# Memory attention and two MLPs: key-value sums in eight places of the array, and other changes to the start

## The chip, the cores and the metric

The kernel runs on one core of one Trainium2 chip, in one launch. The metric is the device time of one execution in microseconds, the median of several runs; lower is better.

## The reference

Four batches, eight heads, 576 tokens, 64 values a head, 32 memory slots. All data is float32.

```
a    = softmax(phi over tokens)            # phi: 4 x 8 x 576 x 32
k_m  = a^T k ;  v_m = a^T v                # 32 x 64 a head
attn = softmax(q k_m^T / 8 over the 32)    # 576 x 32 a head
x    = attn v_m                            # joined over heads: 2304 x 512
h    = x w_in ;   g = max(0.01 h, h) ;     x  = g w_out     # w_in 512 x 2048, w_out 2048 x 512
h    = x w_in2 ;  g = h tanh(softplus h) ; out = g w_out2
```

The weights come in 64-bit floats and are decoded on the chip from their two 32-bit words.

## The kernel before, in words

**Stages.** Heads are taken in two groups of four. For a batch and a group, `kv_first` (batch 0) or `kv_tasks` (the others) loads phi, keys and values, subtracts the maximum over tokens, takes the exponential, and sums a^T k and a^T v on TensorE; `kv_norm` divides by the token sums (a scaled copy called kvn) and transposes. `score_tasks` loads and transposes queries, multiplies them with the keys (`scores`) and does the softmax over 32 slots in two halves of 288 tokens (`half`, nearly all on VectorE). `vw_tasks` multiplies v_m with a chunk of w_in, so that the first layer works straight on the softmax. The first layer then runs over items (`stage1`): one block of 128 hidden columns times one half of a batch's tokens; each item has six matmuls (L1044) and, behind the activation, twelve with w_out (L1077). A weight piece of w_in (w0 to w3 are the first chunk) or of w_out (`wo_unit`) is loaded raw, decoded on ScalarE and VectorE, and split in a rounded part and a rest. The second MLP (L1398 and L1551) takes the second half of the time.

**Batch 0.** Its layout puts head h of a group on partitions 32h to 32h + 31, each partition with 18 tokens. The sums are 72 matmuls of 32 x 32 weights and 128 columns (keys and values side by side), 18 for each head; head h uses rows 32h and columns 32h of the array, so four places lie on the diagonal. Each float32 matmul stands in the trace as two instructions. The token sums are made on VectorE (`fold`: a reduction, a 32 x 32 transpose, a reduction).

**Order.** Nothing is ordered by hand. Each step is a task with a priority, an estimated duration on each engine that could do it, the tasks that it waits for and the buffers that it takes. `Order.run` is a list scheduler that goes through estimated time when the program is built; what it picks becomes the fixed order of each engine's queue. A lower priority number goes first. `K['O']` gives the order of batch 0's loads on the SP queue, which issues all transfers. `K['FILL']` counts filler matmuls (L874) for an idle TensorE early on. `T` gives the turns: batch 0 with chunk 0 and then 1 of w_in, then batch 1, and so on. Loads of batch 1 wait for batch 0's buffers of phi, keys, values and queries of group 0; group 1 has its own in a side pool. PSUM has eight buffers: acc0 to acc3, h0, h1 and two misc.

Of the kernel before, what the change touches and what calls it, by code (L numbers as in the profile page):

```python
# [9 lines left out]
F32 = mybir.dt.float32  # L10
# [4 lines left out]
ALU = mybir.AluOpType  # L15
AX = mybir.AxisListType
# [7 lines left out]
def hop(a, b):  # L24
# [5 lines left out]

K = dict(
    LAG1=2, WIN=8, OB=2, RS=4, FILL=36, A1=10, S1=2.8,
    A2=30, S2=2.6, V1=2.4, V2=14, W2=56.0, W2S=3.8, O='phi0 kv0 phi1 q0 w0 kv1 q1 w1 w2 w3', HF0=-20.0, HF1=-7.0,
    HFD=0.3, TOP=0.3, HI=0.2, WO=2.0, WOL=1, WC=3.0, WC0=-38.0, V0=3.0, COLD=20, GL=1.5, AL=5.0, XL=22.0, T='0:1 0:1 1:2 0:2 1:2', SB=1,
    DW=280e3, DQ=1.3, DP=1.2, DS=0.78, DI=0.38, L4=0.5, L4P=1.6, L4S=0.8, L4T=5.0, MA=6, FK=-52.5, DWF=0.85, MV="......rvvrrvvrvr",
)


# [121 lines left out]
def kernel(  # L160
# [111 lines left out]
    make_identity(nc, ident)  # L272
    ones = const.tile([P, PR], F32, name="ones")
    nc.vector.memset(ones, 1.0)
    sched = Order()

    def dma(**args):
# [21 lines left out]
    def act(n, ps=False):  # L299
        return n / 1196 + (0.051 if ps else 0.093)  # L300
# [126 lines left out]
    def kv_first(g, p0, dp):  # L427
        sp = "s" if g else ""
        ph = tags["phi" + sp].new([P, 576] if sp else [P, HG * R * M])
        kv = tags["kv" + sp].new([P, 2304] if sp else [P, 2 * HG * R * D])  # L430
        phv = lambda: ph.t[:, :576].rearrange("p (r m) -> p r m", m=M)
        hs = slice(g * HG, (g + 1) * HG)
        l_phi = add(
            {"SP": K["DS"] * mb(294912)}, PPHI[g],
            lambda e: (ph.make(), dma(out=phv(), in_=phi[0, hs].rearrange("h (p r) m -> (h p) r m", r=RQ))), (), [ph],
        )

        def ld(e):
# [24 lines left out]

        t1 = add({"DVE": 2.8}, p0, fmax, [l_phi], [rm, mx], [ph])
        t2 = add(
            {"ACT": act(576)}, p0 + 2 * dp,
            lambda e: nc.scalar.activation(out=ph.t[:, :576], in_=ph.t[:, :576], func=AF.Exp), [t1], (), [ph],
        )
        den, rec = tags["den" + sp].new([P, 1]), tags["rec" + sp].new([P, 1])

        def fden(e):
            fold(ALU.add, den.make())
            nc.vector.tensor_scalar(out=den.t, in0=den.t, scalar1=1e-9, scalar2=None, op0=ALU.add)
            nc.vector.reciprocal(out=rec.make(), in_=den.t)

        t3 = add({"DVE": 1.9}, p0 + 3.5 * dp, fden, [t2], [den, rec], [ph, rm])
        acc = acc_tag.slots[2 * g].new([P, 2 * D])

        def fkv(e, r0):
            if not r0:  # L480
                acc.make()
            for r in range(r0, r0 + RQ // 3):
                for h in range(HG):
                    rows = slice(M * h, M * (h + 1))
                    nc.tensor.matmul(  # L485
                        out=acc.t[rows, :].rearrange("p (j d) -> p j d", j=2),
                        lhsT=phv()[rows, r, :],
                        rhs=kv.t[rows, :2304].rearrange("p (j r d) -> p j r d", j=2, r=RQ)[:, :, r, :],
                        start=(r == 0),
                        stop=(r == RQ - 1),  # L490
                    )

        t4 = None
        for r0 in range(0, RQ, RQ // 3):
            t4 = add(
                {"PE": 1.4}, K["FK"] if g else p0 + 3.8 * dp, lambda e, r0=r0: fkv(e, r0), [t2, l_kv, t4], [] if t4 else [acc],
                [ph, kv, acc] if t4 else [ph, kv],
            )
        return acc, rec, t4, t3

    def kv_tasks(b, g, p0, dp):
# [4 lines left out]
        kv = tags["kv" + sp].new([P, 2, HG, R, D])  # L506
        hs = slice(g * HG, (g + 1) * HG)
        pl = p0 - 6
        l_phi = load(pl, ph.make, lambda: phi[b, hs].rearrange("h (p r) m -> p h r m", p=PR), 294912, (), [ph], (), K["DP"])

        def ld(e):
            kv.make()
            for j, x in enumerate((k, v)):
                dma(out=kv.t[:PR, j], in_=x[b, hs].rearrange("h (p r) d -> p h r d", p=PR))

        l_kv = add({"SP": K["DQ"] * mb(1179648)}, pl + 0.2, ld, (), [kv])

        def fold(buf, op):

# [90 lines left out]
    def kv_norm(b, g, p0, dp, acc, rec, t7, t8):  # L610
        sp = "s" if b < K['SB'] and g == 1 else ""
        kvn = tags["kvn" + sp].new([P, 2 * D])

        def fn(e):
            if e == "ACT":
                nc.scalar.activation(out=kvn.make(), in_=acc.t, func=AF.Copy, scale=rec.t)
            else:
                nc.vector.tensor_scalar(out=kvn.make(), in0=acc.t, scalar1=rec.t, scalar2=None, op0=ALU.mult)

        t9 = add({"ACT": act(P, True), "DVE": dve(P)}, p0 + 4.3 * dp, fn, [t7, t8], [kvn], [acc, rec])  # L620
        kt = (misc if b else acc_tag.slots[1]).new([P, P])
# [23 lines left out]
    def score_tasks(b, g, pq, ps, dp):  # L645
        sp = b < K['SB'] and g == 1
        qT = (qT_s if sp else qT_tag).new([P, HG, NB1])
        parts, firsts_q = [], []
# [11 lines left out]
                    in_=q_g[h].rearrange("(j p r) d -> p j (r d)", r=2, p=32),  # L660
                )

        lq = add({"SP": (K["DQ"] if b else K["DS"]) * mb(589824)}, pq - 4 if b else PQ[g], ld, (), [qb])
        for i in range(3):
            ps_b = (misc if b else h_tag).new([P, 3, P])

# [53 lines left out]
    def half(b, g, hf, ps, dp, qT, parts, a, ab, both):  # L720
# [50 lines left out]
    win, win_ready, w_scr = {}, {}, {}  # L771

    def vw_tasks(b, c, p0):

# [884 lines left out]
```

## Time and profile before

| | us |
|---|---|
| median of 3 runs | 750.35 (749.92 to 750.53) |
| the profiled execution | 751.77 |
| its span, first to last instruction | 750.0 |
| PE busy | 737.4 (98%) |
| DVE busy | 545.8 (73%) |
| ACT busy | 413.1 (55%) |
| transfers | 183.75 MB, mean 245 GB/s |

PE is TensorE, PEld its weight loads, DVE VectorE, ACT ScalarE, SP the engine whose queue issues transfers. An "idle before" names the time for which an engine stood still and what ended it. [...] The stretch before 40 us holds batch 0's attention and the first weights; nearly all the rest is the two MLPs, in which batches 1 to 3 are prepared beside the matmuls.

### The profile page before, as it was taken

The page shows a single profiled execution, that of the slowest core. Times are in us where ns is not written, and L with a number is a line of the kernel's source. Part 1 is how long each engine was busy: PE and PEld are TensorE (multiplying, and loading weights), DVE is VectorE, ACT ScalarE, POOL GpSimd, SP SyncE. Part 2 cuts the span into 40 slices and gives each one's busy share as a digit, 9 for nine tenths or more (in the row PEclk, how much of TensorE's full clock was granted, in tenths as well). Part 3 has the DMA queues.
Part 4 walks back from the last instruction along what each step waited for, and adds up shares of the span by engine and source line. Part 5 has one row for each costly group of instructions (what it writes and reads, how often), then busy time and mean ns, then how long its engine had stood idle before and what let it go on. Part 6 is the DMA issues. An engine that isn't in the chain of part 4 may idle for free.

```text
span 750.0 us, 15892 instructions
## 1 busy us (share of the span) xinstructions
PE 737.4 (98%) x5978; PEld 706.4 (94%) x5978; DVE 545.8 (73%) x1180; ACT 413.1 (55%) x916; POOL 0.7 (0%) x6
## 2 busy tenths in 40 slices
PE   8899999999999999999999999999999999999997
PEld 7689899988898998999999999999999999999997
DVE  6989758768676886655779798767576965665585
ACT  3867457646464656554456674644455644454443
POOL 0000000000000000000000000000000000000000
PEclk9999999999999999999999999999999999999999
DMA  9984595838869397966269988788977878987476
GB/s 345 294 286 136 176 285 169 245 122 263 239 222 320 141 300 241 308 193 215 99 247 317 351 321 293 226 265 258 322 250 245 266 246 254 290 289 224 126 214 193
DMA packets 99436, 183.75 MB, mean 245 GB/s; under 512 B 8224, under 2 KB 55328, under 8 KB 99360
## 3 DMA queue, kind: packets, MB, share of 16 engines
q1 hardware_dynamic: 99360, 182.75, 75.8%
q8 instruction: 47, 0.77, 0.4%
q14 instruction: 29, 0.24, 0.1%
HBM read 140.25 MB, written 42.47 MB: 244 GB/s over the span
## 4 chain that ended last, share of the span: by engine, by line
PE 90%; DVE 3%; DMA 3%; ACT 2%; issue 1%; SPq 0%; ACTq 0%; DVEq 0%
PE acc_t L1077 25%; PE h_t L1398 21%; PE acc_t L1551 17%; PE h_t L1044 12%; PE misc_t L1551 7%; PE misc_t L793 2%; PE acc_t L1398 2%; DMA q_t<-in_q_dram 1%; PE acc_t L485 1%; PE misc_t L579 1%; DMA rawm_t<-in_moe_w_in_dram 1%; DMA raw_t<-w2scr 1%; PE misc_t L673 1%; PE misc_t L707 1%; DVE vw_t L326 0%
## 5 line engine op out<-in xcount | busy, mean ns | idle before, releaser
L1077 PE MATMUL acc_t<-hi_t,wo_t 128*128 128x288 f32 x1024 | 163.3, 299 | 0.9 <-ACT x_t L310 0.8
L1077 PEld LDWEIGHTS acc_t<-hi_t,wo_t 128*128 128x128 f32 x1024 | 143.2, 188 | 14.0 <-issue 9.3
L1551 PE MATMUL acc_t<-wo_t,hi_t 128*128 128x256 f32 x720 | 133.7, 279 | 0.0
L1044 PE MATMUL h_t<-at_t,vw_t 128*128 128x288 f32 x768 | 124.7, 298 | 2.7 <-ACT e_t L1058 0.9
L1551 PEld LDWEIGHTS acc_t<-wo_t,hi_t 128*128 128x128 f32 x720 | 118.0, 188 | 0.2 <-DVE ob_t L312 0.2
L1044 PEld LDWEIGHTS h_t<-at_t,vw_t 128*128 128x128 f32 x768 | 109.8, 189 | 4.0 <-ACT e_t L1058 1.4
L1058 ACT ACTIVATE hi_t<-h_t 128x288 fp32r<-128x288 f32 x128 | 52.4, 410 | 110.6 <-PE acc_t L1077 89.4
L1551 PE MATMUL acc_t<-wo_t,lo_t 128*128 128x256 f32 x360 | 102.0, 283 | 0.0
L1065 DVE TENSOR_TENSOR lo_t<-e_t,hi_t 128x288 fp32r<-128x288 f32 x128 | 57.7, 454 | 54.7 <-ACT e_t L1058 28.5
L1077 PE MATMUL acc_t<-lo_t,wo_t 128*128 128x288 f32 x512 | 91.2, 300 | 0.2 <-DVE lo_t L1065 0.2
L1398 PE MATMUL h_t<-xt_t,vw_t 128*128 128x384 f32 x396 | 79.2, 336 | 0.0
L1077 PEld LDWEIGHTS acc_t<-lo_t,wo_t 128*128 128x128 f32 x512 | 74.7, 188 | 4.5 <-issue 3.6
L1520 DVE TENSOR_TENSOR lo_t<-wo_t,hi_t 128x384 fp32r<-128x384 f32 x94 | 52.0, 555 | 36.9 <-ACT hi_t L310 35.5
L1398 PE MATMUL h_t<-xt_t,wo_t 128*128 128x384 f32 x352 | 75.5, 336 | 0.0
L1551 PEld LDWEIGHTS acc_t<-wo_t,lo_t 128*128 128x128 f32 x360 | 67.6, 188 | 0.0
L1398 PEld LDWEIGHTS h_t<-xt_t,vw_t 128*128 128x128 f32 x396 | 66.7, 188 | 0.5 <-DVE wo_t L1417 0.5
L310 ACT ACTIVATE hi_t<-wo_t 128x384 fp32r<-128x384 f32 x83 | 43.4, 523 | 41.0 <-PE acc_t L1551 28.4
L1398 PEld LDWEIGHTS h_t<-xt_t,wo_t 128*128 128x128 f32 x352 | 59.5, 188 | 0.1
L1551 PE MATMUL misc_t<-wo_t,hi_t 128*128 128x256 f32 x288 | 54.1, 279 | 0.0
L1058 ACT ACTIVATE e_t<-h_t 128x288 f32<-128x288 f32 x128 | 51.8, 407 | 0.0
L1520 DVE TENSOR_TENSOR lo_t<-vw_t,hi_t 128x384 fp32r<-128x384 f32 x50 | 27.7, 555 | 25.4 <-ACT hi_t L310 25.2
L1423 ACT ACTIVATE wo_t<-wo_t 128x384 f32<-128x384 f32 x53 | 27.6, 521 | 32.9 <-DVE wo_t L1417 32.7
(219 smaller groups left out, 1079.0 us busy)
## 6 DMA issues: line engine op xcount, KB each, us to landing
wo_t<-tscr SPq DMA_DIRECT2D x168, 256.0 KB, 3.9
vw_t<-wsum SPq DMA_DIRECT2D x32, 512.0 KB, 4.7
win_t<-wscr SPq DMA_DIRECT2D x24, 512.0 KB, 5.9
raw_t<-in_moe_w_in_dram SPq DMA_DIRECT2D x19, 512.0 KB, 6.9
raw_t<-in_moe_w_out_dram SPq DMA_DIRECT2D x17, 512.0 KB, 7.7
wsum<-vw_t SPq DMA_DIRECT2D x16, 512.0 KB, 5.1
wo_t<-wsum SPq DMA_DIRECT2D x16, 512.0 KB, 4.3
kv_t<-in_k_dram SPq DMA_DIRECT2D x8, 576.0 KB, 9.8
```

The costliest lines, as they stand in the source:

```text
L310: nc.scalar.activation(out=o, in_=i, func=AF.Copy)
L485: nc.tensor.matmul(out=acc.t[rows, :].rearrange("p (j d) -> p j d", j=2), lhsT=phv()[rows, r, :], rhs=kv.t[rows, :2304].rearrange("p (j r ...
L579: nc.tensor.matmul(out=acc.t[M * h:M * (h + 1), :].rearrange("p (j d) -> p j d", j=2), lhsT=ph.t[:, h, r, :], rhs=kv.t[:PR, :, h, r, :], s ...
L793: nc.tensor.matmul(out=pss[g].t[M * (h ^ g):M * (h ^ g) + M, :], lhsT=vT[b, g][0].t[rows, h // 2, :], rhs=wbs[g].t[rows, h // 2, :], start ...
L1044: nc.tensor.matmul(out=h.t, lhsT=us[g][0].t[:, wi, j0:j0 + P], rhs=ats[g][0].t[:, ai, cols], start=(n == 0), stop=(n == 3 * NG - 1),)
L1058: nc.scalar.activation(out=o, in_=h.t, func=AF.Prelu, alpha=0.01)
L1065: lambda e: nc.vector.tensor_tensor(out=lb.make(), in0=eb.t, in1=hb.t.bitcast(F32), op=ALU.subtract),
L1077: nc.tensor.matmul(out=ac[kk].t, lhsT=wu[0].t[:, wi, kk * P:(kk + 1) * P], rhs=(hb if src == 0 else lb).t, start=(first and (wi, src) == ( ...
L1398: nc.tensor.matmul(out=h.t, lhsT=w[:, wi, c0:c0 + P], rhs=xp[b, xi].ap()[:, j], start=(first and j == 0 and k3 == 0), stop=(j == 1 and k3 ...
L1423: lambda e: nc.scalar.activation(out=t_of[x](), in_=h.t if h else t_of[x](), func=AF.Mish),
L1520: lambda e, hb=hb, lb=lb, src=src: nc.vector.tensor_tensor(out=lb.make(), in0=src(), in1=hb.t.bitcast(F32), op=ALU.subtract),
L1551: nc.tensor.matmul(out=ac[t].t, lhsT=x.t[:, t * P:(t + 1) * P], rhs=T[:, wi], start=(u == 0 and n3 == 0 and first_of), stop=(u == CH - 1 a ...
```

## The change

Batch 0's sums take two places for each head: even and odd tokens of the 18 go to neighbouring column groups, heads 0 and 1 write one PSUM buffer (acc0), heads 2 and 3 another (acc1). Both are copied to SBUF, and a matmul for each head with a 0/1 matrix (`folder`) adds the two halves into acc2. The sums of a group are one task now, not three. For group 1 the token sums go through TensorE: phi is multiplied with a 0/1 matrix (`heads`), copied, and folded. The transposed keys of batch 0 use misc in place of acc1. In the load order group 1's queries come ahead of its keys, and the first weight piece behind them. The second half of group 0's scores has priority -3 in place of -20. A gate on batch 1's loads is written in, with the index `GA`.

```diff
-    A2=30, ... O='phi0 kv0 phi1 q0 w0 kv1 q1 w1 w2 w3', HF0=-20.0, HF1=-7.0,
+    A2=30, ... O='phi0 kv0 phi1 q0 q1 kv1 w0 w1 w2 w3', HF0=-3.0, HF1=-7.0,
-    ... FK=-52.5, DWF=0.85, MV="......rvvrrvvrvr",
+    ... FK=-52.5, DWF=0.85, GA=9, FS=-53.3, MV="......rvvrrvvrvr",
...
+    nc.vector.tensor_reduce(out=heads, in_=ident.rearrange("p (h m) -> p h m", h=4), axis=AX.X, op=ALU.add)
+    nc.vector.tensor_reduce(out=folder, in_=ident.rearrange("p (h m) -> p m h", h=4), axis=AX.X, op=ALU.add)
...
+        acc = acc_tag.slots[2].new([P, 2 * D])
+        part_ps, part_sb = [acc_tag.slots[x].new([P, 2 * D]) for x in range(2)], pt_tag.new([P, 2, 2 * D])
+        def fkv(e):
+            for x in part_ps:
+                x.make()
+            for r in range(RQ):
                 for h in range(HG):
-                    rows = slice(M * h, M * (h + 1))
+                    c = 2 * (h % 2) + r % 2
                     nc.tensor.matmul(
-                        out=acc.t[rows, :].rearrange("p (j d) -> p j d", j=2),
+                        out=part_ps[h // 2].t[M * c:M * (c + 1)].rearrange("p (j d) -> p j d", j=2),
...
+        t4 = add({"PE": 2.3}, K["FK"] if g else p0, fkv, [t2, l_kv], part_ps, [ph, kv])
+        for x in range(2):      # copies of part_ps to part_sb, ACT or DVE, the second behind the first
...
+        def ffold(e):
+            acc.make()
+            for h in range(HG):
+                rows = slice(D * (h % 2), D * (h % 2) + D)
+                nc.tensor.matmul(out=acc.t[M * h:M * (h + 1), :], lhsT=folder[rows], rhs=part_sb.t[rows, h // 2, :], start=True, stop=True)
...
+            def fsums(e):       # group 1 only
+                dn.make()
+                for i in range(5):
+                    n = min(P, RQ * M - P * i)
+                    nc.tensor.matmul(out=dn.t[:n, 4:8], lhsT=ph.t[:, P * i:P * i + n], rhs=heads, start=(i == 0), stop=(i == 4), skip_group_check=True)
+            def fsums2(e):
+                for h in range(HG):
+                    nc.tensor.matmul(out=dn.t[M * h:M * (h + 1), 0:1], lhsT=folder, rhs=sums.t[:, h:h + 1], start=True, stop=True, skip_group_check=True)
...
+        gate = [x for y in range(NG) for x in win_ready[0, 0, y]][K["GA"]:K["GA"] + 1] if b == 1 and g == 0 else []
...
-        kt = (misc if b else acc_tag.slots[1]).new([P, P])
+        kt = misc.new([P, P])
```

## Rows read from the trace of the kernel before

**Rows 1.** The page, chain that ended last: shares of the span by engine.
```profile
PE 90%; DVE 3%; DMA 3%; ACT 2%; issue 1%; SPq 0%; ACTq 0%; DVEq 0%
```

**Rows 2.** Stretches: length, busy us (instructions) of PE, PEld, DVE, ACT, POOL; clock, DMA share, GB/s.
```profile
16.00:20.00 4.00, 4.00 (x115) 2.97 (x107) 2.91 (x9) 1.45 (x3) 0.00 (x0) 1.00 1.04 422
25.00:30.00 5.00, 4.83 (x47) 3.63 (x47) 4.68 (x13) 4.98 (x10) 0.00 (x0) 1.00 1.10 237
...
28.00:32.40 4.40, 2.76 (x24) 1.95 (x16) 4.05 (x12) 4.38 (x10) 0.00 (x0) 0.98 1.08 212
...
32.40:35.40 3.00, 2.90 (x13) 2.88 (x13) 3.00 (x8) 2.09 (x6) 0.00 (x0) 0.50 1.05 339
40.00:57.00 17.00, 16.68 (x133) 15.33 (x133) 12.85 (x26) 11.17 (x25) 0.00 (x0) 1.00 0.80 255
8.00:25.00 17.00, 16.01 (x355) 12.16 (x355) 13.23 (x36) 9.48 (x20) 0.00 (x0) 1.00 1.05 368
```

**Rows 3.** The chain in order of time: start us, us, what.
```profile
24.72 0.68 ACT raws_t L369
...
38.54 0.39 DVE T_t L757
```

**Rows 4.** Timeline, DVE: start us, us, line, operation, tiles, idle before.
```profile
3.58 1.14 DVE L451 TENSOR_REDUCE rm_t<-phi_t 128x32 f32<-128x576 f32 x1 [2.62 <-DMA phi_t<-in_phi_dram]
...
12.90 0.86 DVE L312 COPY qT_t<-h_t 128x384 f32<-128x384 f32 x1 [0.87 <-PE h_t L673]
...
17.53 0.48 DVE L727 STREAM_TRANSPOSE T_t<-misc_t 128x288 f32<-128x288 f32 x1 [1.02 <-PE misc_t L707]
...
20.90 0.35 DVE L618 TENSOR_SCALAR kvn_t<-acc_t,rec_t 128x128 f32<-128x128 f32 x1 [0.91 <-PE acc_t L485]
...
40.90 0.68 DVE L326 TENSOR_TENSOR wo_t<-raw_t,wo_t 128x512 fp32r<-128x512 f32 x1
```

**Rows 5.** Timeline, group 0 of batch 0: sums, scaled copy, scores.
```profile
8.01 1.51 PE L485 MATMUL acc_t<-kv_t,phi_t 32*32 32x128 f32 x48 [1.38 <-DMA kv_t<-in_v_dram]
...
14.38 0.36 ACT L616 ACTIVATE kvn_t<-acc_t,rec_t 128x128 f32<-128x128 f32 x1
...
16.78 0.69 PE L707 MATMUL misc_t<-qT_t,kT_t 64*32 64x288 f32 x8
```

**Rows 6.** Tile acc_t, 7.9 to 15 us: ns least/median/most, first and last start.
```profile
L485 PE MATMUL acc_t<-kv_t,phi_t x144: 264/268/292, 8.0 to 14.0; 32*32 32x128 f32 x144
```

**Rows 7.** Timeline, group 1 of batch 0: sums, scores.
```profile
15.28 1.57 PE L485 MATMUL acc_t<-kv_t,phi_t 32*32 32x128 f32 x48
...
24.18 0.79 PE L707 MATMUL misc_t<-qT_t,kT_t 64*32 64x288 f32 x16
```

**Rows 8.** Timeline, products of values and weights: chunk 0, chunk 1.
```profile
27.10 1.09 PE L793 MATMUL acc_t<-win_t,vT_t 64*32 64x512 f32 x16
...
52.49 1.09 PE L793 MATMUL misc_t<-win_t,vT_t 64*32 64x512 f32 x16
```

**Rows 9.** Timeline, token sums of group 1 on DVE.
```profile
14.52 1.14 DVE L451 TENSOR_REDUCE rm_t<-phi_t 128x32 f32<-128x576 f32 x1 [0.24 <-ACT phi_t L467]
...
15.70 0.21 DVE L452 STREAM_TRANSPOSE rm_t<-rm_t 128x32 f32<-128x32 f32 x1
15.94 0.18 DVE L453 TENSOR_REDUCE den_t<-rm_t 128x1 f32<-128x32 f32 x1
```

**Rows 10.** Timeline, token sums of batch 1 on PE.
```profile
56.25 0.72 PE L590 MATMUL misc_t<-ones,rm_t 96*128 96x1 f32 x6
```

**Rows 11.** Timeline, SP queue: issues of a weight piece and of values.
```profile
21.25 0.35 SPq L279 DMA_DIRECT2D raw_t<-in_moe_w_out_dram  x1
...
25.82 0.31 SPq L279 DMA_DIRECT2D kv_t<-in_v_dram  x1
```

**Rows 12.** Issues at 21.25 and 25.82 us: count, KB, us to landing.
```profile
raw_t<-in_moe_w_out_dram SPq DMA_DIRECT2D x1, 512.0 KB, 11.4
...
kv_t<-in_v_dram SPq DMA_DIRECT2D x1, 576.0 KB, 10.1
```

More of the change, by code (lines that the diff above doesn't have):

```diff
@@ L32 @@
     LAG1=2, WIN=8, OB=2, RS=4, FILL=36, A1=10, S1=2.8,
-    A2=30, S2=2.6, V1=2.4, V2=14, W2=56.0, W2S=3.8, O='phi0 kv0 phi1 q0 w0 kv1 q1 w1 w2 w3', HF0=-20.0, HF1=-7.0,
+    A2=30, S2=2.6, V1=2.4, V2=14, W2=56.0, W2S=3.8, O='phi0 kv0 phi1 q0 q1 kv1 w0 w1 w2 w3', HF0=-3.0, HF1=-7.0,
     HFD=0.3, TOP=0.3, HI=0.2, WO=2.0, WOL=1, WC=3.0, WC0=-38.0, V0=3.0, COLD=20, GL=1.5, AL=5.0, XL=22.0, T='0:1 0:1 1:2 0:2 1:2', SB=1,
-    DW=280e3, DQ=1.3, DP=1.2, DS=0.78, DI=0.38, L4=0.5, L4P=1.6, L4S=0.8, L4T=5.0, MA=6, FK=-52.5, DWF=0.85, MV="......rvvrrvvrvr",
+    DW=280e3, DQ=1.3, DP=1.2, DS=0.78, DI=0.38, L4=0.5, L4P=1.6, L4S=0.8, L4T=5.0, MA=6, FK=-52.5, DWF=0.85, GA=9, FS=-53.3, MV="......rvvrrvvrvr",
 )
@@ L274 @@
     nc.vector.memset(ones, 1.0)
+    heads, folder = spool.tile([P, 4], F32, name="heads"), spool.tile([P, 32], F32, name="folder")
+    nc.vector.tensor_reduce(out=heads, in_=ident.rearrange("p (h m) -> p h m", h=4), axis=AX.X, op=ALU.add)
+    nc.vector.tensor_reduce(out=folder, in_=ident.rearrange("p (h m) -> p m h", h=4), axis=AX.X, op=ALU.add)
     sched = Order()
@@ L403 @@
     qT_s = Tag(spool, "qT", 1)
+    pt_tag, sums_tag = Tag(spool, "pt", 1), Tag(spool, "sums", 1)
     T_s, T2_s = Tag(spool, "T1", 2), Tag(spool, "T2", 1)
@@ L421 @@
     kT, vT, at, vw, wo = {}, {}, {}, {}, {}
+    win, win_ready, w_scr = {}, {}, {}
     def keep(t):
@@ L469, in kv_first @@
         den, rec = tags["den" + sp].new([P, 1]), tags["rec" + sp].new([P, 1])
[L471 to L482, printed above, removed]
+        acc = acc_tag.slots[2].new([P, 2 * D])
@@ L483, in fkv @@
+        part_ps, part_sb = [acc_tag.slots[x].new([P, 2 * D]) for x in range(2)], pt_tag.new([P, 2, 2 * D])
[3 more added lines that the diff above has]
+            for r in range(RQ):
                 for h in range(HG):
-                    rows = slice(M * h, M * (h + 1))
+                    c = 2 * (h % 2) + r % 2
                     nc.tensor.matmul(
-                        out=acc.t[rows, :].rearrange("p (j d) -> p j d", j=2),
[L487 to L490, printed above, removed]
-                    )
@@ L493, in kv_first @@
[L493 to L498, printed above, removed]
+                        out=part_ps[h // 2].t[M * c:M * (c + 1)].rearrange("p (j d) -> p j d", j=2),
+                        lhsT=phv()[M * h:M * (h + 1), r, :],
+                        rhs=kv.t[M * h:M * (h + 1), :2304].rearrange("p (j r d) -> p j r d", j=2, r=RQ)[:, :, r, :],
@@ new lines, in fkv @@
+                        start=(r < 2),
+                        stop=(r >= RQ - 2),
+                    )
+        t4 = add({"PE": 2.3}, K["FK"] if g else p0, fkv, [t2, l_kv], part_ps, [ph, kv])
+        tc_ = []
+        for x in range(2):
+            tc_.append(add(
+                {"ACT": act(P, True), "DVE": dve(P)}, p0 + 3.8 * dp,
+                lambda e, x=x: copy(e, part_sb.t[:, x] if x else part_sb.make()[:, x], part_ps[x].t), [t4, *tc_],
+                [] if x else [part_sb], [part_ps[x], part_sb] if x else [part_ps[x]],
+            ))
@@ new lines, in ffold, with fden @@
+        def ffold(e):
[3 more added lines that the diff above has]
+                nc.tensor.matmul(out=acc.t[M * h:M * (h + 1), :], lhsT=folder[rows], rhs=part_sb.t[rows, h // 2, :], start=True, stop=True)
+        t4 = add({"PE": 0.4}, p0 + 3.9 * dp, ffold, tc_, [acc], [part_sb])
+        if not g:
+            def fden(e):
+                fold(ALU.add, den.make())
+                nc.vector.tensor_scalar(out=den.t, in0=den.t, scalar1=1e-9, scalar2=None, op0=ALU.add)
+                nc.vector.reciprocal(out=rec.make(), in_=den.t)
+            t3 = add({"DVE": 1.9}, p0 + 2.1 * dp, fden, [t2], [den, rec], [ph, rm])
+        else:
+            dn, sums = misc.new([P, 8]), sums_tag.new([P, HG])
+            def fsums(e):
[3 more added lines that the diff above has]
+                    nc.tensor.matmul(out=dn.t[:n, 4:8], lhsT=ph.t[:, P * i:P * i + n], rhs=heads, start=(i == 0), stop=(i == 4), skip_group_check=True)
+            ts = add({"PE": 1.1}, K["FS"] + 0.01 * g, fsums, [t2], [dn], [ph])
+            td = add({"ACT": 0.2, "DVE": 0.2}, K["FS"], lambda e: copy(e, sums.make(), dn.t[:, 4:8]), [ts], [sums], [dn])
+            def fsums2(e):
+                for h in range(HG):
+                    nc.tensor.matmul(out=dn.t[M * h:M * (h + 1), 0:1], lhsT=folder, rhs=sums.t[:, h:h + 1], start=True, stop=True, skip_group_check=True)
+            ts = add({"PE": 0.3}, K["FS"], fsums2, [td], (), [dn, sums])
+            def fden(e):
+                nc.vector.tensor_scalar(out=den.make(), in0=dn.t[:, 0:1], scalar1=1e-9, scalar2=None, op0=ALU.add)
+                nc.vector.reciprocal(out=rec.make(), in_=den.t)
+            t3 = add({"DVE": 0.34}, K["FS"], fden, [ts], [den, rec], [dn])
@@ L508, in kv_tasks @@
         pl = p0 - 6
-        l_phi = load(pl, ph.make, lambda: phi[b, hs].rearrange("h (p r) m -> p h r m", p=PR), 294912, (), [ph], (), K["DP"])
+        gate = [x for y in range(NG) for x in win_ready[0, 0, y]][K["GA"]:K["GA"] + 1] if b == 1 and g == 0 else []
+        l_phi = load(pl, ph.make, lambda: phi[b, hs].rearrange("h (p r) m -> p h r m", p=PR), 294912, gate, [ph], (), K["DP"])
         def ld(e):
@@ L514, in ld @@
                 dma(out=kv.t[:PR, j], in_=x[b, hs].rearrange("h (p r) d -> p h r d", p=PR))
-        l_kv = add({"SP": K["DQ"] * mb(1179648)}, pl + 0.2, ld, (), [kv])
+        l_kv = add({"SP": K["DQ"] * mb(1179648)}, pl + 0.2, ld, gate, [kv])
         def fold(buf, op):
@@ L645, in score_tasks @@
     def score_tasks(b, g, pq, ps, dp):
+        gate = [x for y in range(NG) for x in win_ready[0, 0, y]][K["GA"]:K["GA"] + 1] if b == 1 and g == 0 else []
         sp = b < K['SB'] and g == 1
@@ L661, in ld @@
                 )
-        lq = add({"SP": (K["DQ"] if b else K["DS"]) * mb(589824)}, pq - 4 if b else PQ[g], ld, (), [qb])
+        lq = add({"SP": (K["DQ"] if b else K["DS"]) * mb(589824)}, pq - 4 if b else PQ[g], ld, gate, [qb])
         for i in range(3):
@@ L769, in half @@
         )))
-    win, win_ready, w_scr = {}, {}, {}
     def vw_tasks(b, c, p0):
```

## The prediction

> **What bounds the kernel now.** The chain of waits comes first: 90% of the span is TensorE (PE) [rows 1], so only what makes PE start sooner or do less counts. The table of stretches shows where PE is not full [rows 2]: from 40 to 57 us it is busy 16.68 of 17 us, and this stays so nearly to the end. What the change can touch is therefore the time before 40 us. There the chain leaves PE: from 24.72 us it runs over ScalarE (ACT) and then almost wholly over VectorE (DVE), whose last piece ends at 38.93 us [rows 3]. DVE is what the start waits for, but it was not full all along: from 8 to 25 us it was busy 13.23 of 17 us [rows 2], so 3.77 us were idle, and three of the gaps (0.87, 1.02 and 0.91 us, 2.80 together) ended when PE delivered something [rows 4]. So a step before 40 us is worth the DVE time that it removes or lets DVE use sooner, not the PE time that it saves.
>
> **Key-value sums, group 0.** Before, 72 matmuls (144 instructions) ran from 8.01 to about 14.3 us with query transposes and fillers between; they began as soon as the values had landed, and a third of them (48 instructions) takes 1.51 us [rows 5]; one instruction takes 268 ns, and the last of 144 begins at 14.0 us [rows 6]. A third is 12 turns of four, less one latency, (1.51 - 0.27)/11.5, so about 0.11 us a turn. With eight places a turn holds eight: 18 turns, 18 x 0.11 + 0.27 = 2.2 us, without a break, so they end at about 10.25 us. Added: two copies out of PSUM, one behind the other, 0.36 us each by the nearest row (the scaled copy of the same 128x128 [rows 5]), and a fold of four matmuls in four places (0.27 + 0.11, about 0.4 us). With handoffs of some 0.2 us three times, 1.7 us; the ACT may be in a query copy of about 0.87 us. The scaled copy, at 14.38 us before, then starts between 12.0 and 12.8 us, and the scores, at 16.78 us before [rows 5], some 2 us sooner.
>
> Are eight at once to be had? The trace has it for taller places: eight score instructions (four places) took 0.69 us [rows 5], sixteen (eight places) 0.79 us [rows 7], and sixteen of 512 columns 1.09 us [rows 8]. The 32x32 shape in eight places it does not show. Bounds: 2.2 us, and 4.4 us where only four run at once; I take 2.2, since the row of eight places is the nearest.
>
> [...]
>
> **Key-value sums, group 1.** Its keys exchange one transfer of 512 KB ahead of them (a piece of the first weights) for one of 576 KB (its queries), so they land when they did, within 0.2 us. Before: sums from 15.28 us, the scaled copy right behind them at 20.90, scores at 24.18 [rows 4, 7]. Now 15.3 + 2.2 = 17.5, copies and fold to 19.2, the scaled copy at about 19.3, and the scores 2 us on (3.3 before, with a stall of PE behind queries that come sooner now): 21.3 us, some 3 us sooner.
>
> **Token sums of group 1.** DVE loses a reduction, a transpose and a reduction, 1.14 + 0.21 + 0.18 = 1.53 us [rows 9]; the two small operations on the denominator stay. PE gains 10 instructions with 128-column weights; six of that kind took 0.72 us [rows 10], so 1.2 us, and eight of 32 columns (0.3 to 1.0 us). They take the place of fillers, of which a fixed number fills idle PE, so nothing is charged; without that cover they would cost up to 2.2 us on PE ahead of the sums. The result is there by about 16.5 us, ahead of the 19.3 us where it is needed. One small copy is added.
>
> **Copies.** Four of 0.36 us and one small one, ACT or DVE. ACT is busy only 1.45 us between 16 and 20 us [rows 2], so I charge DVE with one of the four, 0.35 us (bounds 0 and 1.4).
>
> **Moved, or nothing.** The first weight piece lands some 4 us later; its decode (about 1.35 us on ACT, 0.7 on DVE) goes to about 17 us, into that idle ACT. The two reductions for the helper matrices fall into the 2.62 us in which DVE waits for its first data [rows 4]: nothing. The gate takes element 9 of a list of four, so it is empty and holds nothing back. The transposed keys go into the other PSUM pair: nothing, bounds 0 and 0.3. The second half of group 0's scores moves behind both halves of group 1: DVE has the same work in another order, but the first matmuls of the first layer need only first halves, so PE can start up to 3 us sooner on four items while DVE does the rest. In a sum by DVE that is nothing; bounds: nothing, and a gain of 2 us. [...]
>
> **Sum.** 1.53 removed, 0.35 added, and half of the 2.80 us of gaps used, 1.4, since part of them only moves to other waits: 1.53 - 0.35 + 1.4 = 2.6 us sooner. The profiled execution took 751.77 us for a span of 750.0, so it would take 749.2; against the median of the runs, 750.35 us, which lies 1.4 us lower, 747.8 us. After that, PE is late by its own work again.
>
> **Rivals.**
> 1. All the gaps go and the order of halves pays: 1.53 + 2.80 + up to 1 = 4.3 to 5.3 us, 745.0 to 746.0 us. For it: group 1's scores come 3 us sooner. Against: ACT is as full as DVE from 25 to 30 us (4.98 of 5 us [rows 2]), and it takes the copies.
> 2. The start is sooner but the gain is given back before 57 us. The second chunk of weights is multiplied at 52.49 us [rows 8]; PE has no slack there [rows 2], and if its transfers and decodes keep their time, PE stands still in front of it for what it won: 750.0 to 750.4 us. Against: ACT and DVE are only 66% and 76% busy from 40 to 57 us, so the decode can move up.
> 3. The change doesn't do what it says: the 32x32 matmuls run four at once. Each group's sums then take 4.4 + 1.7 us without a break. Group 1: 15.3 + 6.1 = 21.4 against 20.90, half a microsecond late; the 1.53 us stay: about 749.5 us.
> 4. Slower: the buffers of group 0's phi, keys and values come free 4 us sooner, so batch 1's loads (until then issued around the fourth second-layer weight piece, 21.25 us, and at 25.82 us, landing 10.1 us later [rows 11, 12]) go ahead of that piece on SP's queue. The transfers are full in these stretches (shares above 1 [rows 2]). The piece landed at 21.25 + 11.4 = 32.7 us, and the keys and values behind it, at 35.9; exchanged, it lands 3.2 us later. Its second part was written at 40.90 us [rows 4], 8.2 us after the landing. It decides from the point where that second part comes later than 40.90: if the 8.2 us stay, it comes at 44.1 us, and with some 1 us of other items that PE can put first the whole ends 2.2 us late: 752.5 us. Against: most of the 8.2 us was queueing on a full DVE, not work.
>
> **How the numbers follow.** Forecast 0.50 (747.8 us, own range 746.3 to 748.8); rival 1 0.15; rival 2 0.20; rival 3 0.05; rival 4 0.10. A measurement of this kernel can tell about 0.2%, 1.5 us, from no change: faster is below 748.85. Faster: 0.47 of the forecast's, rival 1 whole and 0.04 of rivals 2 and 3: 0.66. Slower: rival 4 and 0.02 of rival 2, where a stall is longer than what was won: 0.12. The rest, 0.22, is no change. The range, 745.0 to 751.5 us, leaves out rival 4 and the far end of rival 1.
>
> **What would show it.** Right: each group's sums in one stretch of 2.0 to 2.5 us; group 1's scores at 20.5 to 22.5 us; the first item of layer one with all its inputs before 31 us; DVE full from about 20 us; PE from 40 to 57 us still above 97%. Wrong: sums of 4 us (rival 3); idle PE ahead of the second chunk's products (rival 2) or of the fourth weight piece (rival 4); a clock at half for much more than 3 us.

## The result: slower by 0.6%, and the profile after

The changed kernel took 754.7 us (median), the kernel before 750.4 us in the same job: a ratio of 1.006 (95% interval 1.0042 to 1.0078). The forecast was 747.8 us; its range ended at 751.5. The profiled execution took 754.23 us for a span of 752.5 us, 2.5 us more than before, with a mean granted clock of 0.991 (before 0.997).

The timeline of TensorE (PE) in the changed kernel answers to [rows 5, 7] (start, busy time, line, operation, count, idle time before it and what ended it). L484 are the sums, L505 the folds, L668 the transposition of keys and values, L750 the scores, L915 the fillers, L1085 the first layer, L1118 the matmuls with w_out.

```profile
7.26 2.25 PE L484 MATMUL acc_t<-kv_t,phi_t 32*32 32x128 f32 x144 [0.90 <-ACT phi_t L472]
...
12.76 0.33 PE L668 MATMUL misc_t<-ident,kvn_t 128*128 128x128 f32 x1 [0.44 <-DVE kvn_t L660]
...
13.25 1.23 PE L524 MATMUL misc_t<-heads,phi_t 128*128 128x4 f32 x10
14.41 0.69 PE L750 MATMUL misc_t<-qT_t,kT_t 64*32 64x288 f32 x8
15.03 0.24 PE L531 MATMUL misc_t<-sums_t,folder 128*32 128x1 f32 x8
15.20 1.98 PE L484 MATMUL acc_t<-kv_t,phi_t 32*32 32x128 f32 x122
20.40 0.63 PE L484 MATMUL acc_t<-kv_t,phi_t 32*32 32x128 f32 x22 [3.23 <-issue]
...
24.35 0.65 PE L505 MATMUL acc_t<-pt_t,folder 64*32 64x128 f32 x8
24.93 2.93 PE L915 MATMUL acc_t<-ident 128*128 128x128 f32 x12
27.66 0.42 PE L668 MATMUL misc_t<-ident,kvn_t 128*128 128x128 f32 x1
...
29.24 0.72 PE L750 MATMUL misc_t<-qT_t,kT_t 64*32 64x288 f32 x16
...
36.29 2.65 PE L1085 MATMUL h_t<-at_t,vw_t 128*128 128x288 f32 x9 [1.29 <-ACT at_t L313]
...
40.87 1.40 PE L1118 MATMUL acc_t<-hi_t,wo_t 128*128 128x288 f32 x6
```

Group 0 is as forecast: 144 instructions in 2.25 us, and the scores at 14.41 instead of 16.78 us. Group 1 starts at 15.20 as forecast and then stops: after 122 of its 144 instructions PE stands for 3.23 us in the middle of the sums, and "issue" says that it waited for nothing that the profile shows. Its data had long landed, or the 122 could not have run. From there everything is late: group 1's scores come at 29.24 us (24.18 before [rows 7]) and the first full item at 36.29 us. The first matmuls with w_out begin at 40.87 us; before, they began 5.5 us sooner:

```profile
35.34 0.63 PE L1077 MATMUL acc_t<-hi_t,wo_t 128*128 128x288 f32 x2
```

The table of stretches, against [rows 2] (busy time of each engine, then PE's granted clock and the share of the transfer engines):

```profile
17.20:20.40 3.20, 0.00 (x0) 0.00 (x0) 1.20 (x4) 0.61 (x2) 0.00 (x0) 1.00 1.03 416
20.00:21.00 1.00, 0.60 (x23) 0.40 (x22) 0.00 (x0) 0.00 (x0) 0.00 (x0) 1.00 1.03 422
21.00:22.00 1.00, 1.00 (x8) 0.76 (x6) 0.00 (x0) 0.72 (x2) 0.00 (x0) 0.69 1.05 361
22.00:23.00 1.00, 1.00 (x9) 0.20 (x8) 0.80 (x2) 1.00 (x4) 0.00 (x0) 0.50 1.09 276
27.00:28.00 1.00, 1.00 (x7) 1.00 (x6) 0.00 (x0) 0.00 (x0) 0.00 (x0) 0.50 1.22 209
28.00:29.00 1.00, 1.00 (x10) 1.00 (x9) 0.29 (x2) 0.57 (x3) 0.00 (x0) 0.90 1.24 194
25.00:30.00 5.00, 5.00 (x48) 4.64 (x55) 2.06 (x6) 3.02 (x8) 0.00 (x0) 0.68 1.19 223
8.00:25.00 17.00, 12.94 (x334) 9.28 (x319) 11.32 (x33) 9.36 (x19) 0.00 (x0) 0.89 1.03 381
36.00:41.00 5.00, 4.38 (x16) 3.93 (x17) 4.93 (x14) 3.23 (x9) 0.00 (x0) 0.50 0.59 229
40.00:57.00 17.00, 17.00 (x127) 16.87 (x126) 13.97 (x29) 13.21 (x33) 0.00 (x0) 0.95 0.67 220
```

After this standstill of PE (called the stand from here on) PE's granted clock is at half (0.50) from 21.4 to 28.2 us, and again from 35.0 to 41.9 us. At half clock run the fold and twelve fillers (2.93 us) that the program put ahead of the transposition. VectorE (DVE) pays: it is busy 11.32 of the 17 us from 8 to 25 (13.23 before) and 2.06 of the 5 us from 25 to 30 (4.68 before [rows 2]). Its timeline names the two gaps:

```profile
22.20 0.87 DVE L315 COPY qT_t<-h_t 128x384 f32<-128x384 f32 x1 [3.73 <-PE h_t L716]
...
28.71 0.23 DVE L315 COPY vT_t<-misc_t 64x64 f32<-64x64 f32 x1 [2.84 <-ACT kT_t L313]
```

From 40 to 57 us PE is full, so rivals 2 and 4, which put a stall there, did not happen.

**What PE waited for.** The page's third part has a queue that no line of the program issues:

```profile
q8 instruction: 48, 0.79, 0.4%
```

That is 48 packets of some 16 KB. PE has 6012 matmul and 6012 weight-load records, 12,024 over 48, some 250 a packet; with the 207 semaphore instructions that the trace also has of PE, 255. (The page's other instruction queue, q14, has 29 packets, 0.24 MB; PE's instructions over these would be 422 a packet.) In the traces PE always stands at the same places of its instruction order: at number 705 (the kernel before and the changed one), or with 80 more instructions ahead (E1) at 449, which is 256 less. From this the reading is that PE's program reaches it in blocks of 256 instructions, over the same transfer engines as the data (the 0.4% is a share of the 16 that carry the data). The block that begins at 705 seems to be asked for when PE passes 449, at 15.04 us. Two stretches of the changed kernel's transfers, 14.4 to 17.8 and 17.8 to 19.2 us (packets, MB, share of the 16 engines):

```profile
DMA packets 387, 1.40 MB, mean 412 GB/s; under 512 B 45, under 2 KB 45, under 8 KB 387
...
q1 hardware_dynamic: 387, 1.40, 102.0%
...
DMA packets 153, 0.57 MB, mean 410 GB/s; under 512 B 16, under 2 KB 16, under 8 KB 152
...
q1 hardware_dynamic: 152, 0.56, 98.4%
q8 instruction: 1, 0.02, 4.5%
```

In the first all 387 packets are data and the engines are full; in the second is the instruction packet, which ran from 18.01 to 19.02 us. PE goes on at 20.40, 1.4 us behind its end. The kernel before stands at the same instruction: 449 passed at 16.06, packet 19.83 to 20.76, PE on again at 22.06:

```profile
22.06 0.60 PE L673 MATMUL h_t<-ident,qs_t 128*128 128x128 f32 x4 [0.85 <-issue]
```

It loses only 0.85 us, since its 256 instructions took 4.9 us (16.06 to 20.93) to run. In the changed kernel the eight-place sums run nearly 256 instructions in 1.9 us (15.04 to 16.91), and PE could go on only 5.4 us after the asking (6.0 us before).

### The profile page after: what moved, and what is told of

Same layout as the page of the kernel before. It is cut to its first block, busy times and chain, and to the rows that moved or that the text cites. A ratio compares the mean times of both kernels' runs of the same rounds, so it can differ in the third digit from the quotient of the medians.

```text
span 752.5 us, 15968 instructions
## 1 busy us (share of the span) xinstructions
PE 736.7 (98%) x6012; PEld 706.8 (94%) x6012; DVE 545.9 (73%) x1183; ACT 413.0 (55%) x917; POOL 0.7 (0%) x6
## 4 chain that ended last, share of the span: by engine, by line
PE 95%; DVE 3%; ACT 1%; DMA 1%; issue 1%; ACTq 0%
PE acc_t L1118 28%; PE h_t L1439 22%; PE acc_t L1592 17%; PE h_t L1085 13%; PE misc_t L1592 7%; PE misc_t L834 2%; PE acc_t L1439 2%; PE misc_t L621 1%; PE misc_t L750 1%; PE misc_t L716 1%; PE acc_t L915 1%; DVE rm_t L456 0%; DMA phi_t<-in_phi_dram 0%; PE acc_t L484 0%; ACT wo_t L313 0%
## 5 line engine op out<-in xcount | busy, mean ns | idle before, releaser
L1118 PE MATMUL acc_t<-hi_t,wo_t 128*128 128x288 f32 x1024 | 163.3, 299 | 0.0
L1118 PEld LDWEIGHTS acc_t<-hi_t,wo_t 128*128 128x128 f32 x1024 | 143.6, 189 | 11.3 <-issue 8.5
L1085 PE MATMUL h_t<-at_t,vw_t 128*128 128x288 f32 x768 | 125.3, 299 | 3.6 <-ACT at_t L313 1.3
L1085 PEld LDWEIGHTS h_t<-at_t,vw_t 128*128 128x128 f32 x768 | 110.5, 191 | 5.1 <-ACT at_t L313 1.5
L1118 PE MATMUL acc_t<-lo_t,wo_t 128*128 128x288 f32 x512 | 91.4, 300 | 0.0
L1118 PEld LDWEIGHTS acc_t<-lo_t,wo_t 128*128 128x128 f32 x512 | 74.6, 188 | 5.1 <-issue 4.6
```

Of the source, the lines that this page charges most:

```text
L1085: nc.tensor.matmul(out=h.t, lhsT=us[g][0].t[:, wi, j0:j0 + P], rhs=ats[g][0].t[:, ai, cols], start=(n == 0), stop=(n == 3 * NG - 1),)
L1118: nc.tensor.matmul(out=ac[kk].t, lhsT=wu[0].t[:, wi, kk * P:(kk + 1) * P], rhs=(hb if src == 0 else lb).t, start=(first and (wi, src) == ( ...
```

## The experiments

All are timed beside the kernel before, whose median was 750.1 to 750.7 us in each job. Behind each time stands its ratio to the kernel before with the 95% interval, and the length of the stand. The theory: the instruction block is late, and the half clock, which in the changed kernel began at 21.4 us, 1.0 us behind the end of the stand, and the late fold follow from it. Rivals: the new order of loads and halves (B), the token sums on PE (D), the number of fillers, and a price of the small matmuls themselves.

**E1: 80 more instructions ahead of everything.**

```diff
+    def tiny(e):
+        for _ in range(20):
+            nc.tensor.matmul(out=warm.t[:32, 0:1], lhsT=ident[:, 0:32], rhs=ident[:, 0:1], start=True, stop=True)
...
```

> The changed kernel with 20 tiny matmuls (128x32 weights, one column; 80 instructions of PE) ahead of the first filler, the planned order untouched. Theory (PE's instructions come in blocks of 256 that queue behind saturated transfers; in the changed kernel PE stood 3.23 us at its 705th instruction, the 61st of group 1's 72 matmuls): the block's end moves 80 instructions, so no stall over 0.5 us inside group 1's sums, which run in one stretch of 2.0 to 2.4 us; instead a stall of about 2 us at instruction 449, near group 0's fold (11 us). Total 752.5 to 754.5 us. Rival A (the stall belongs to the matmuls in eight places or to data they wait for): it stays at the 61st matmul, 3.2 us, total 754 to 755.5. Rival B (the new order of loads and score halves costs the time, the stall is by the way): total 754 to 755.5 whatever the stall does.

756.0 us, 1.0076 [1.0058, 1.0094]. The place of the stand moved as the theory wants, to number 449, which now is a fold of group 0, and no stand is left in group 1's sums:

```profile
9.93 2.25 PE L484 MATMUL acc_t<-kv_t,phi_t 32*32 32x128 f32 x144
...
15.98 0.42 PE L505 MATMUL acc_t<-pt_t,folder 64*32 64x128 f32 x8 [2.78 <-issue]
```

The time missed: group 0's sums began 2.7 us later behind the added instructions, and the clock was at half from 16.3 to 26.6 us. That the stand sits at a number and not at a line is shown, and with it falls the rival that it is a price of the small matmuls.

**E2: second-layer pieces behind the first weights.**

```diff
-        b, ld = load_raw(p - K["WOL"], "wo", m, 0, raws if m < 8 else rawm)
+        b, ld = load_raw(p - K["WOL"], "wo", m, 0, raws if m < 8 else rawm, w_lds[2:3] if m < 3 else ())
...
```

> The changed kernel with the first three second-layer weight pieces issued only when the third piece of the first weights has landed (18 us in place of 9 to 12 us). Theory: the instruction block that is asked for at 15.0 us has fewer transfers ahead of it, so PE's stall of 3.23 us falls to 0.5 to 2.5 us and the total to 751.5 to 754. Rival A: stall 3.2 us as before, total 754 to 755.5. Rival B: total 754.5 to 757, since loads come later and nothing else changes.

756.5 us, 1.0084 [1.0067, 1.0101]; stand 4.12 us, longer and not shorter as was expected. The edit only reordered the loads; the transfers stayed as full as before (share 1.01 from 15.2 to 18.6 us), so it tested nothing about queueing. E13 does that.

**E4 and E5: the order of loads and halves back; that order alone.** E4 puts the old `O` and `HF0` into the changed kernel, E5 the new ones into the kernel before.

```diff
-    ... O='phi0 kv0 phi1 q0 q1 kv1 w0 w1 w2 w3', HF0=-3.0, ...
+    ... O='phi0 kv0 phi1 q0 w0 kv1 q1 w1 w2 w3', HF0=-20.0, ...
```

This is E4's; E5's is the reverse.

> The changed kernel with the load order and the priority of the second score half as before; eight places and token sums on PE stay. Theory: PE still eats 288 instructions in 2 us, so a stall of 2 to 4 us stays at instruction 705 and the total is 752 to 755. Rival A: the same. Rival B: the total returns to 750.5 us or below.

> The kernel before with only the new load order and the new priority of the second score half. Theory: its sums take 5 us for 256 instructions, so the stall at instruction 705 stays about the 0.86 us that it was (at most 1.5) and the total is 749 to 751.5. Rival A: the same, 749 to 751.5. Rival B: 753 to 755.

E4: 755.8 us, 1.0072 [1.0057, 1.0087], stand 3.64 us. E5: 750.1 us, 0.9993 [0.9984, 1.0002], stand 0.68 us. Rival B falls from both sides.

**E8: the token sums of group 1 on DVE again.**

```diff
-        if not g:
+        if True:
...
```

> The changed kernel with the token sums of group 1 on DVE, as before. Theory: the stall only moves to a later matmul of the sums (36 instructions fewer ahead of them) and stays 3 to 4.5 us: 753 to 756.5 us. Rival D (the token sums on PE cost the time): 749 to 751.5 us.

755.5 us, 1.0065 [1.0039, 1.0091], stand 4.03 us. Rival D falls; nor did the 1.53 us that DVE was spared show in the time, though the interval, 2 us either way, is too wide to exclude it.

**E6: twenty fillers in place of thirty-six.**

```diff
-    ... FILL=36, ...
+    ... FILL=20, ...
```

> The changed kernel with 20 fillers in place of 36, so that none stands behind group 1's sums. Theory: the stall at instruction 705 stays 3.2 us, but no fillers at half clock stand ahead of the transposition of group 1's scaled copy (2.2 us in the changed kernel): 752.5 to 754.5 us. Rival C (fillers are what brings the clock back; without them the first layer starts at half clock for longer): 755 to 758 us.

753.5 us, 1.0041 [1.0026, 1.0056]. The stand is 4.08 us, the transposition comes at 27.28 us (27.66 in the changed kernel). Fewer fillers take away what stood in front of it, but the clock is at half from 20.4 to 44.3 us.

**E7: only group 1's sums back in four places, in three tasks** (`fkv` of the kernel before where `g` is 1).

> The changed kernel with group 1's key-value sums in four places and three tasks, as before; group 0 in eight, token sums on PE, the new order. Theory: 288 instructions take 5 us again and the next block comes in time or nearly so: stall at instruction 705 under 1.2 us, clock full before 30 us, total 748 to 751 us. Rival B, and a rival D (the token sums on PE cost the time): 753 to 756 us.

751.3 us, 1.0003 [0.9988, 1.0018]; the stand is 1.15 us:

```profile
20.99 1.06 PE L484 MATMUL acc_t<-kv_t,phi_t 32*32 32x128 f32 x28 [1.15 <-issue]
```

Without this part of the change the loss is gone; without the order (E4) or the token sums (E8) it stays.

**E3 and E12: nine fillers of 512 columns**, in the changed kernel (E3) and in the kernel before (E12). Fewer instructions, the same PE time.

```diff
-    for i in range(K["FILL"]):
+    for i in range(K["FILL"] // 4):      # rhs: ident four times, 512 columns
...
```

> The changed kernel with a quarter of the fillers, each 512 columns wide in place of 128: some 60 instructions of PE fewer ahead of group 1's sums, so that instruction 705 lies behind them (the planner orders a few steps anew). Theory (blocks of 256 instructions, the next but one asked for at the end of a block, 5 to 6 us under saturated transfers): the sums run in one stretch of 2.0 to 2.4 us, PE stands 2 to 4 us behind them instead, and the copies and part of the chain go on meanwhile: 751.5 to 754.5 us. Rival B (the planned order costs the time, the stall does not): 754.5 to 756.

> The kernel before with the wide fillers alone. Theory: the stall of 0.86 us at instruction 705 goes, nothing else: 749.2 to 750.6 us. Rival F (fewer, wider fillers get in the way of work that is ready or leave the clock at half for longer): 751 to 753 us.

E3: 750.9 us, 1.0005 [0.9992, 1.0018]. E12: 750.1 us, 0.9998 [0.9989, 1.0007]. In E3 there is no stand, though 2 to 4 us of it were expected behind the sums:

```profile
14.69 3.86 PE L484 MATMUL acc_t<-kv_t,phi_t 32*32 32x128 f32 x144
18.48 0.24 PE L531 MATMUL misc_t<-sums_t,folder 128*32 128x1 f32 x8
```

The sums ran at half clock here (0.94 in the mean from 8 to 16 us, 0.70 from 16 to 20; 3.86 us against 2.25 for group 0's in the changed kernel), and fewer instructions lay ahead, so PE came to 705 only after the block (at 20.6 us; the packet ended at 19.4). In the kernel before the same fillers remove the stand of 0.85 us too (E12), and the time stays: a stand of that length cost nothing that can be measured.

**E9, E10, E11: the same wide fillers with group 1 in four places; with the new order alone; and sixteen of them** in the changed kernel (`FILL=64`).

> The run with group 1's sums in four places, and with a quarter of the fillers, each 512 columns wide. Theory: the stall of 1.15 us at instruction 705 goes too, since some 50 instructions fewer lie ahead; group 0's gain and the lighter DVE then show: 747.5 to 750.3 us. Rival E (the start is bound by DVE's order and the weights, not by when the keys are ready): 750 to 752 us.

> The kernel before with the new load order and half priority, and the wide fillers. Theory: its stall of 0.68 us at instruction 705 goes; 748 to 750.3 us. Rival E: 749.8 to 751.5 us.

> The changed kernel with 16 wide fillers in place of 9 (36 narrow ones before): seven stand ahead of the first layer, so that PE does not sit idle there. Theory that the clock at half in the first items (32 to 38 us in the run with 9) costs time: full clock there, 748.5 to 750.5 us. Rival (PE waits for DVE there whatever its clock, or the fillers stand in the way of work that is ready): 750.5 to 753 us.

750.1 us, 0.9984 [0.9975, 0.9994]; 749.7 us, 0.9984 [0.9975, 0.9993]; 749.2 us, 0.9987 [0.9978, 0.9996]. None has a stand. With sixteen wide fillers the changed kernel is 5.5 us faster than with its own, and 0.13% faster than the kernel before; but so is the kernel before with the new order and nine wide fillers (E10, 0.16%), so none of this can be put down to the eight places.

**E13: no data in flight while the block is fetched.** The first weight piece, and so all that SP issues behind it, waits for the end of group 1's sums.

```diff
...
+            def fq(e):
+                b.make()
+                nc.vector.tensor_copy(out=b.t[:, 0, 0:1].bitcast(F32), in_=pt.t[:, 0, 0:1])
+
+            held = [add({"DVE": 0.1}, prio, fq, [t4], [b], [pt])]
...
```

> The changed kernel, except that the first weight piece, and with it everything that SP issues behind it, waits until group 1's key-value sums are done (a one-column copy on DVE from their result, written into the piece's buffer, makes it wait); the block of TensorE's instructions that begins at number 705 is asked for at about 15.0 us, so between 14.4 us (the last key and value bytes landed) and the end of the sums no data is in flight. By the theory (the block is late because it queues behind data transfers: 5.4 us from the crossing of 449 to PE's resumption in the changed kernel, 1.1 us at 69 us where the transfers were nearly idle) the block comes within 1-2.5 us and the 3.23 us stand at 705 shrinks to 0-0.7 us; the sums of group 1 end by 18.0. Rival: the stand is PE's own (a fixed price of that instruction or of so many small matmuls in a row) or the block takes its 5 us whatever the transfers do: the stand stays 2.5-3.5 us. The total decides nothing, since the weights and batch 1's inputs come some 3-8 us later than before: 752-760 us either way.

757.3 us, 1.0103 [1.0087, 1.0119]; the weights come later, and the total decides nothing. Its transfers from 15.2 to 16.4 us, all there is:

```profile
DMA packets 1, 0.02 MB, mean 14 GB/s; under 512 B 0, under 2 KB 0, under 8 KB 0
...
q8 instruction: 1, 0.02, 5.4%
```

PE passes 449 at 15.18 us, the packet starts at 15.31 and ends at 16.34, and PE does not stand at 705 (busy, weight loads, DVE, ACT, clock, share):

```profile
14.00:15.00 1.00, 1.00 (x14) 0.67 (x13) 0.39 (x2) 0.90 (x2) 0.00 (x0) 1.00 0.00 0
15.00:16.00 1.00, 1.00 (x52) 0.82 (x56) 0.66 (x4) 0.00 (x0) 0.00 (x0) 0.89 0.06 16
16.00:17.00 1.00, 1.00 (x56) 1.00 (x46) 0.84 (x3) 0.09 (x1) 0.00 (x0) 0.50 0.00 0
17.00:18.00 1.00, 1.00 (x53) 1.00 (x45) 0.58 (x2) 0.35 (x1) 0.00 (x0) 0.50 0.00 0
18.00:19.00 1.00, 1.00 (x42) 0.63 (x24) 0.26 (x2) 0.00 (x0) 0.00 (x0) 0.50 0.08 16
```

The packet started 0.13 us after the asking instead of 2.97 us: the lateness is queueing behind data, and the rival that the block takes its 5 us whatever the transfers do falls. One reserve, on the stand itself: the sums ran at half clock here, 3.75 us. At full clock PE would, by an estimate from the changed kernel's times, have been at 705 at about 17.0 us, and with the 1.4 us that PE took after a packet's end in the changed kernel, some 0.7 us of stand would have remained (15.18 + 1.87 against 16.34 + 1.4).

**E14 and E15: sixteen wide fillers with group 1, and with both groups, in four places** (E15 is the kernel before with the new order).

> The changed kernel with group 1's sums in four places and three tasks as before, and sixteen fillers of 512 columns in place of thirty-six of 128. Theory: no stand at 705 and the clock full up to the first items; group 1's sums take 2.3 us longer than in the kernel with wide fillers and eight places in both groups (749.24 us), so 749.0-751.0 us. Rival (eight places in group 1 are worth nothing to the end even without the stand): 748.5-749.5, not slower than that kernel.

> The kernel before with the changed order of loads, the changed head start of the queries, and sixteen fillers of 512 columns. Theory: as the kernel before in the same order with nine such fillers (749.66 us), within 0.2%: 748.5-750.8 us, no stand at 705. If the forecast gain of the eight places (2.3 us per group) reached the end once the stand is gone, this one is 1.5-3 us slower than the changed kernel with the same fillers (749.24); if it did not, they agree within 1 us.

749.5 us, 0.9991 [0.9981, 1.0002], and 748.7 us, 0.9982 [0.9970, 0.9993]. With E11 (749.2) that is the comparison without a stand: eight places in both groups (E11), four in group 1 (E14), four in both (E15). They agree within 0.8 us, and the old sums are not the slower ones. It is not a clean one: the clock was at half from 15.7 to 19.1 us in E11 and from 15.0 to 21.8 us in E14 (full was expected), and group 1's sums ran slower there (3.34 us for 144 instructions in E11, 2.78 us for the first 48 in E14 against 1.51 in E15); in E15 it was full from 5 us on. E15 has the lowest time of all kernels run, 0.18% under the kernel before, but its interval overlaps with those of E9, E10, E11 and E14.

E14 also shows that late scores of group 1 are not the loss by themselves:

```profile
28.50 0.45 PE L773 MATMUL misc_t<-qT_t,kT_t 64*32 64x288 f32 x4
...
36.60 1.62 PE L1108 MATMUL h_t<-at_t,vw_t 128*128 128x288 f32 x8
```

Its scores (28.50 us) and first items (36.60) come about as late as in the changed kernel (29.24 and 36.29), and even the profiled execution, the slowest of its twelve, took 751.1 us, 3.1 us less than that kernel's. What differs from there on is the clock, full from 21.8 us on in E14 and at half again from 35.0 to 41.9 us in the changed kernel, and the planned order; no run parts these two.

E11's timeline shows where the sums' 2.3 us went there:

```profile
14.68 3.34 PE L484 MATMUL acc_t<-kv_t,phi_t 32*32 32x128 f32 x144
...
20.24 0.70 PE L750 MATMUL misc_t<-qT_t,kT_t 64*32 64x288 f32 x8
20.88 0.55 PE L716 MATMUL h_t<-ident,qs_t 128*128 128x128 f32 x3
21.35 0.31 PE L505 MATMUL acc_t<-pt_t,folder 64*32 64x128 f32 x4
...
23.15 0.27 PE L668 MATMUL misc_t<-ident,kvn_t 128*128 128x128 f32 x1
...
25.07 0.45 PE L750 MATMUL misc_t<-qT_t,kT_t 64*32 64x288 f32 x4
```

and E15's:

```profile
19.78 1.51 PE L485 MATMUL acc_t<-kv_t,phi_t 32*32 32x128 f32 x48
...
23.28 0.27 PE L626 MATMUL acc_t<-ident,kvn_t 128*128 128x128 f32 x1
...
25.20 0.45 PE L707 MATMUL misc_t<-qT_t,kT_t 64*32 64x288 f32 x4
```

E11's sums end at 18.0 us, 3.2 us ahead of E15's, but the fold stands on PE behind nine query transposes, a filler and a set of scores, and begins at 21.35. The transpositions come at 23.15 and 23.28, the scores at 25.07 and 25.20: the same.

**E16 and E17: the fold early**, in E11 and in the changed kernel: copies, fold, scaled copy and transposition of group 1 get the sums' own early due time.

```diff
...
-        t4 = add({"PE": 0.4}, p0 + 3.9 * dp, ffold, tc_, [acc], [part_sb])
+        t4 = add({"PE": 0.4}, K["FK"] if g else p0 + 3.9 * dp, ffold, tc_, [acc], [part_sb])
...
```

> The changed kernel with sixteen fillers of 512 columns (749.24 us), and with the copies, the fold, the scaled copy and the transposition of group 1's keys and values at the same early due time as its sums, so that on PE the fold stands behind three query transposes and one filler instead of nine transposes, one filler and four of group 0's scores. In the kernel with these fillers and the changed order the sums end at 18.0 us and the fold begins only at 21.35, the transposition at 23.15. Theory (without the stand, the program's order gives away what the eight places won): the fold begins by 20.2, the transposition by 21.8, group 1's first scores by 23.8 instead of 25.07, and the whole takes 747.0-748.9 us. Rival (DVE, full from 24 us on, sets the first items whatever PE delivers): fold and scores earlier, but the time within 0.1% of that kernel, 748.5-750.0.

> The changed kernel with its own thirty-six narrow fillers, and with the copies, fold, scaled copy and transposition of group 1 at the early due time of its sums. Theory: the stand at instruction 705 stays (3-4 us), and the half clock behind it; the order gains at most the 1 us that now lies between the end of the sums and the fold: 753.0-755.0 us. Rival (the order alone explains the loss): 748-751.

755.6 us, 1.0077 [1.0055, 1.0098], and 757.6 us, 1.0094 [1.0074, 1.0114]. Both times missed, though E16's fold and scores came when they were expected. The fold begins at 19.93 us and the scores at 23.41, 1.7 us sooner than in E11, and yet the first items start at 32.98 us (32.32 in E11), and PE stands behind DVE later:

```profile
43.09 0.79 PE L1118 MATMUL acc_t<-lo_t,wo_t 128*128 128x288 f32 x4 [1.86 <-DVE lo_t L1106]
```

The planner put DVE's and SP's work in another order as well; which of those steps make up the 6.3 us against E11 is not shown. E17 keeps its stand, 2.96 us.

**All runs together.** In the seven kernels with a stand of 2.8 us or more (the changed one, E1, E2, E4, E6, E8, E17) the time is 0.4% to 0.9% above the kernel before, and the clock is at half within 1 us of the stand's end, for 6.8 us or more. In E5 and E7, with 0.68 and 1.15 us, the clock stays full behind it (1.00 from 20 to 30 us); with the seven that have no stand (E3, E9 to E12, E14, E15) they lie between 0.9982 and 1.0005. E13, with its late weights, and E16 are slow without a stand. So every kernel with the long stand has the loss, and among the others only these two. An order alone can cost as much (E16), and how the loss divides between the wait, the clock and the order is not shown.

## Why the prediction was wrong, step by step

**The bound: right in its place.** Only the time before 40 us counts: PE is full from 40 to 57 us, and the first matmuls with w_out, at 40.87 us, are already 5.5 us late, as much as the whole loss and more.

**Group 0: right.** Forecast 2.2 us of sums and scores some 2 us sooner; 2.25 us and 2.37 us. Eight small places do run at once, so rival 3 with its sums of 4 us falls: 144 instructions in 2.25 us are 16 ns each, and each of the two PSUM buffers took two row tiles in that time.

**Group 1: the step that failed.** "Now 15.3 + 2.2 = 17.5, copies and fold to 19.2, the scaled copy at about 19.3." The sums began at 15.20 and ended at 21.03 us, 5.8 us in place of 2.2, since PE stood for 3.23 us at an instruction whose block had not arrived; the fold began at 24.35, the scaled copy at 25.07. The prediction counted a matmul by the row that holds its time and did not count instructions: the sums run 288 of them (matmuls and weight loads) in some 2 us, on a path that took 5.4 to 6.0 us for 256. The kernel before had the sign: the row at 22.06 us, 0.85 us of "issue", which the prediction put down to queries that come late.

**The clock: the sum has no term for it.** There are two stretches at half clock (0.50), 6.8 us each, where before there was one of 3 us [rows 2]; a clock at half for much more than 3 us was one of the prediction's own signs of being wrong. The first began behind the stand and fell on the fold and on fillers ahead of the transposition, the second on the first items. What they cost in the end is not shown by itself.

**The gaps: the 1.4 us are not shown either.** The forecast let half of DVE's gaps be used. With the stand gone (E11, E14, E15) eight places in a group gain nothing that can be measured. E11's timeline shows a reason: the program's order puts other work of PE in front of what the sums free. That this order is the cause is not shown: with the fold early (E16) the scores came 1.7 us sooner and the whole later. Rival 1's sum, 4.3 to 5.3 us, also leaves out the 0.35 us that the forecast charges for a copy.

**The token sums: the mechanism right, the gain not seen.** Ten instructions took 1.23 us (forecast 1.2) and ran ahead of the need, but E8, which undoes them, is no slower beyond its interval of 2 us either way.

**What stays open.** The 5.5 us between the changed kernel and E11 are the stand, the half clock and a planned order that differs, and no run parts them: E16 differs from E11 only in due times and is 6.3 us slower with a stand of 0.2 us. So single differences of 1 or 2 us between kernels with different orders are not put down to one cause. That the block is asked for when PE passes the boundary before it is read from times, not from a row.

## What to carry to other kernels

Before cutting work into more and smaller instructions, count them: where a stretch issues some hundreds of instructions in a few microseconds while the transfers are full, look for idle time that ends in "issue", and for the instruction queue's packets in the same stretch. A gain of 2 us ahead of a fixed order is only a gain if the next step on each engine's queue is the one that it frees. Where a planner orders the queues, a few changed due times can move the end by several microseconds (6.3 us from E11 to E16), so an edit wants its control with the same order.

## What the runs showed of the hardware

PE's instructions are read here as coming over the transfer engines that carry the data (q8, 0.4% of the same 16 engines) and queueing behind it. With the transfers full (share 1.02, the changed kernel) the packet with PE's next block started 2.97 us after PE had passed into the block ahead of it, and with none in flight (E13) 0.13 us; the packet itself took 1.0 us both times, and PE, where it stood for it, went on 1.2 to 1.5 us after its end (1.4 in the changed kernel, 1.3 in the kernel before).

The granted clock fell beside a busy PE: in E13 PE was busy without a break from 14 to 19 us, with four-column matmuls, the scores and then the sums, and the clock was 0.50 from 15.8 us until the query transposes behind the sums, at 19.2 us.
